# Loads of keys and queries, constants and search rounds at other places in an attention and mixture-of-experts kernel

## The chip, the cores and the metric

The kernel runs on one core of a Trainium2 chip. A core has engines that work side by side, each through its own list of instructions in order: TensorE (PE, with its weight loads as PEld), VectorE (DVE), ScalarE (ACT), GpSimd (POOL) and SyncE (SP), which here does nothing but issue DMAs. The metric is the device time of one execution in microseconds (us).

## The reference

Attention over 8 batches of 8 heads, 576 positions and 64 dimensions. Heads 0 to 3 see the last 32 positions (local), heads 4 to 7 every 32nd position (strided). Its output is read as 4608 tokens of 512 values, which 8 experts share out: all token-expert pairs are walked in order of falling logit, and an expert is closed when it has 576 tokens.

```python
    scores = scale * np.matmul(q, k.transpose(0, 1, 3, 2))
    mask_local = (rel >= 0) & (rel < stride)
    mask_strided = (rel >= 0) & (pos[None, :] % stride == pos[:, None] % stride)
    scores = np.where(masks[None, :, :, :], scores, -1000000000.0)
    ...
    return np.matmul(attn, v).astype(np.float32)
```

```python
    cap = N // E
    logits = x @ w_gate
    order = np.argsort(-logits.flatten())
    for idx in order:
        tok, e = (int(idx) // E, int(idx) % E)
        if assigned[tok] >= 0 or counts[e] >= cap:
            continue
        assigned[tok] = e
        counts[e] += 1
    for e in range(E):
        mask = assigned == e
        out[mask] = np.maximum(x[mask] @ w1[e], 0.0) @ w2[e]
```

## The kernel before

**Attention.** The work is cut into 16 units, one for each batch and kind (strided, local, strided, ...); a unit has two pairs of heads, p = 0 and 1. The loop of steps i runs from -1 to 31 (L597). In step i the kernel finishes the scores of pair i + 1 (`close_scores`, `max_t`, `shift`), multiplies the probabilities of pair i with the values (`mix`, L390) and normalizes (`norm`), and opens the scores of pair i + 2 (`open_scores`: `masks` L336, `dots` L347). Four steps make one batch. Gate logits of finished batches, transposes of x and stores of x to a scratch in HBM (`store`, L417 to 429) lie in between. In this part the order on all engines is the order of the code (`tc.manual_schedule()`).

**Loads.** SP issues the loads in the code's order. `flow` (L259) issues a group of transfers; its first one waits for a named instruction (`mark`), or, without a mark, until the group three before has landed. `load_kq` brings the keys and queries of one pair (two transfers of 288 to 304 KB), `load_v` half the values of a unit. Ahead of the loop stand units 0 and 1 in full, the values and the keys and queries of unit 2, and the gate weights. In step i the loop then loads for unit i//2 + 3: half the values at the start of an even step and half in its middle, the keys and queries of pair 0 at its end, of pair 1 in the middle of the odd step. The six constants that routing needs, and desc8h, are issued in step 13 (`CONST_AT`, `late_constants` L169). They are read from `summit` (desc8h, from step 24 on) and from the routing after the loop (the others).

**Routing.** After the last logits the first expert's threshold is found alone (`first_round`, `search0`). An expert is the one that fills up first, so experts are found one after the other: `side` (L1126) searches the threshold of expert ph (`search`), numbers its tokens (`slots`), issues its weight loads (`weights`), starts its index and gather work (`fetch`: `indices`, `tokens`), and strikes its tokens out before the next search. A search has seven rounds. A round compares all logits with 17 thresholds (VectorE `cm` L811), counts by matmul (TensorE L827), sums (VectorE L830, L833), counts again (TensorE L836), compares with the capacity (VectorE L843) and adds up (TensorE L846).

**Experts.** `ffn` (L1177) does the two layers of an expert in float16 halves, L1167 for the first layer, L1209 and L1215 for the second. TensorE's order is written by hand here (`MAN`), that of the other engines comes from a scheduler by priority. All the side work is cut into chains (generators). The planner keeps a clock in ns: each matmul of `ffn` adds its cost (123, 216 or 108), and between two matmuls every chain that is due is taken one step on (L1267 to 1271). What a chain yields is the time until its next step. So in a search T_COUNT = 2950 stands between `cm` and the count L827, T_SUM = 1350 between the count and L836, T_STEP = 1225 between L836 and L846; for the search beside the first expert (one expert closed) they are multiplied by PACE1. T_HOT = 4200 (T_HOT1 = 6350 for ph = 1) stands between the index tables and the index matmul L955. Larger numbers move a matmul later in TensorE's order; too small ones make TensorE wait for the operand.

An expert's `ffn` starts when its chain has set `ready`; the splits of its weights that aren't out by then are put out at once (`rush`). Weights of expert ph are asked for only when `ffn` of ph - 2 is written out (L1132). The split weights have two buffers, the loaded ones one.

Of the kernel before, what the change touches and what calls it, by code (L numbers as in the profile page):

```python
# [19 lines left out]
N, DM, E, FF = B * S, H * D, 8, 1024  # L20
# [8 lines left out]
NB = S // 32  # L29
BANK = 512  # L30
OPEN_S, OPEN_L = 1, 3
CONST_AT = 13
DEPTH = 3
MAX_FIRST = True
WARM = {(-2, 0): 11, (-1, 0): 3, (-1, 2): 3, (31, 0): 2}
# [13 lines left out]
URGENT = 4000  # L49
T_FIRST, T_COUNT, T_SUM, T_STEP, T_PREFIX, T_NEXT, T_HOT, T_DUP, T_LOAD = 1100, 2950, 1350, 1225, 3900, 2300, 4200, 550, 8000  # L50
PACE1 = 0.55
H0 = 256
HURRY = (0, 1, 7)
MAN, MAN0, MANP = {mybir.EngineType.PE}, {mybir.EngineType.Activation}, (0,)
T_W20, T_STEP0 = 9000, 1000
X1 = 100
# [3 lines left out]
T_F, T_LOAD0, T_HOT1, T_W, T_SQ, T_SCALE, T_CUT, T_BULK0 = 3000, 1500, 6350, 4000, 1500, 1500, 1500, 600  # L60
# [77 lines left out]
def band_stride_attention_then_capacity_moe(ctx, tc, qt, kl, ks, nl, ns, wg, w1, w2, cst, out, dbg=None):  # L138
    nc = tc.nc
# [15 lines left out]
    wg_sb = const.tile([128, H // 2, E], F32, name="wg_sb")  # L155
    sum_g = const.tile([128, E], F32, name="sum_g")
# [9 lines left out]
    ones_j = const.tile([128, 128], F16, name="ones_j")  # L166
    nc.vector.memset(ones_j, 1.0)

    def late_constants():  # L169
        for t, name in ((desc8h, "desc_h"), (fold, "fold"), (small, "small"), (tri, "tri"), (pick, "pick"), (iota, "iota")):  # L170
            split_of = {"iota": NC, "pick": 2 * NT}.get(name)
            nc.sync.dma_start(t, cst[name].rearrange("q (s c) -> q s c", c=split_of) if split_of else cst[name])
        nc.sync.dma_start(val[:, :2], cst["val"].rearrange("q (a c) -> q a c", a=2))

    ident_b = const.tile([128, 128], BF16, name="ident_b")
    nc.vector.tensor_copy(ident_b, ident)
# [43 lines left out]
    with tc.tile_pool(name="ld", bufs=2) as ld, \  # L220
# [336 lines left out]
                u.load_v(f)  # L557
        for f in range(2):
            todo[2].load_v(f)
        for p in range(2):  # L560
            todo[2].load_kq(p)
        flow([(wg_sb, wg), (sum_g, cst["sum_g"])])
        last = 2 * nu - 1
        edge = (B - 2) * S // TP

# [31 lines left out]
        for i in range(-1, 2 * nu):  # L597
            u, n, m = pair(i), pair(i + 1), pair(i + 2)
            nu_ = todo[i // 2 + 3] if i >= 0 and i // 2 + 3 < nu else None
            if nu_ and i % 2 == 0:  # L600
                nu_.load_v(0, todo[0].top if i == 0 else todo[i // 2 - 1].done)
            if i == CONST_AT:
                late_constants()
            if n:
                close_scores(n)
            if 2 < i < last:
                x = pair(i - 1)
                x[0].turn(x[1])
            warm(i, 0)
            for f in drips.get(i, []):  # L610
                f()
            for f in squares.get(i, []):
                f()
            if m or i in mids:
                a = room(m) if m else ps_a.tile([128, 2, 512], F32, name="spa")
            if i in mids or i in mids2 or i in mids3:
                b = ps_b.tile([128, 512], F32, name="spb")
            if u:
                if u[1] == 0:
                    u[0].begin()  # L620
                if i < last:
                    u[0].mix(u[1], 0)
            if i < last:
                for f in mids.get(i, []):
                    f(a, b)
            if i == last:
                pt = [ps_a.tile([128, 2, 512], F32, name="spa") for _ in range(2)]
                p1 = ps_b.tile([128, 512], F32, name="spb")
                for ts_, p_ in zip(parts, (None, p1)):
                    for h in range(2):  # L630
                        u[0].mix(u[1], h, ts_, p_)
                    u[0].norm(u[1], ts_, p_)
                break
            if n and MAX_FIRST:
                n[0].max_t(n[1])
            if nu_ and i % 2 == 0:
                nu_.load_v(1, n[0].top)
            elif nu_:
                nu_.load_kq(1, n[0].top)
            if u:  # L640
                u[0].mix(u[1], 1)
            if n and not MAX_FIRST:
                n[0].max_t(n[1])
            warm(i, 1)
            if m:
                open_scores(m)
            warm(i, 2)
            if u:
                u[0].norm(u[1])
            if nu_ and i % 2 == 0:  # L650
                nu_.load_kq(0, u[0].done)
            if i in mids2 and i > 1:
                mids2[i].total_v(b)
            for f in mids3.get(i, []):
                f(a, b)
            if n:
                n[0].shift(n[1])
            warm(i, 3)
            if i == -1:
                todo[0].square_v()  # L660
            if i == 1:
                todo[1].total_v(b)
                todo[1].scale_v()
            if i in FIRST_AT:
                todo[0].turn(FIRST_AT.index(i))
            for f in late.get(i, []) + fills.get(i, []):
                f()
# [129 lines left out]
                    nc.tensor.matmul(pm[:, :E], ones_j[:J], g, start=True, stop=True)  # L797
                    return settle(pm[:, :E], top, grid[:, rd, J0:])

    def pace(t):  # L800
        return t if len(closed) > 1 else t * PACE1

    def search(rm, ohc, more):
        cand, src, top = cand0, rm, None
        ohv = ohc.rearrange("p c e -> p (c e)")
        for rd in range(R1):
            last = rd == R1 - 1
            t = cand[:, :J1] if last else cand[:, 1:J1 + 1]
            with urgent():
                cm = rt.tile([TP, NC, J1], F16, name="cm")  # L810
                nc.vector.tensor_tensor(cm, src[:, :, None].to_broadcast([TP, NC, J1]),  # L811
                                        t[:, None, :].to_broadcast([TP, NC, J1]), op=OP.is_ge)
                cv = cm.rearrange("p c j -> p (c j)")
                n = 1 if rd == R1 - 2 else J1 + 1
                if not last:
                    pre = cand[:, 0:1]
                    if n > 1:
                        pre = rt.tile([128, n], F32, name="pre1")
                        nc.vector.tensor_scalar(pre, steps[:, rd + 1, :n], cand[:, 0:1], None, op0=OP.add)
                if rd == 0:  # L820
                    more()
            yield pace(T_COUNT) + (X1 if len(closed) == 1 else T_FIRST if rd == 0 else 0)
            with urgent():
                pr = ps_r.tile([128, 512], F32, name="pr_")
                pc, p2, pm = pr[:GC * J1, :GC * E], pr[:, 64:64 + E], pr[:, 128:128 + (E if last else 1)]
                for k in range(0, NC, GC):
                    nc.tensor.matmul(pc, cv[:, k * J1:(k + GC) * J1], ohv[:, k * E:(k + GC) * E], start=(k == 0),  # L827
                                     stop=(k == NC - GC))
                red = rt.tile([GC * J1, GC, E], F16, name="red")
                nc.vector.tensor_tensor(red.rearrange("p c e -> p (c e)"), pc, fold[:, :GC * E], op=OP.mult)  # L830
                r8 = rt.tile([GC * J1, E], F16, name="r8")
                with nc.allow_low_precision(reason="whole numbers up to 1152"):
                    nc.vector.tensor_reduce(r8, red.rearrange("p c e -> p e c"), axis=AX.X, op=OP.add)  # L833
            yield pace(T_SUM)
            with urgent():
                nc.tensor.matmul(p2, fold[:, GC * E:], r8, start=True, stop=True, skip_group_check=True)  # L836
                g = rt.tile([128, E], F16, name="g1")
                ih = rt.tile([128, 1], F16, name="ih1")
                if last:
                    nc.vector.tensor_scalar(g, p2, float(CAP), None, op0=OP.is_ge)  # L840
                else:
                    with nc.allow_low_precision(reason="zero or one"):
                        nc.vector.tensor_scalar(g, p2, float(CAP), 0.0, op0=OP.is_ge, op1=OP.max, accum_out=ih)  # L843
            yield pace(T_STEP)
            with urgent():
                nc.tensor.matmul(pm, ones_j, g if last else ih, start=True, stop=True, skip_group_check=True)  # L846
                if not last:
                    cand = rt.tile([128, n], F32, name=f"cand{n}")
                    nc.vector.scalar_tensor_tensor(cand, steps[:, rd, J1 + 1:].to_broadcast([128, n]), pm, pre,
                                                   op0=OP.mult, op1=OP.add)  # L850
                if rd == R1 - 2:
                    top, src = cand, rt.tile([TP, NC], F32, name="rml")
                    nc.vector.tensor_scalar(src, rm, top, None, op0=OP.subtract)
                    cand = steps[:, rd + 1, :J1 + 1]
        with urgent():
            return settle(pm, top, steps[:, R1 - 1, J1 + 1:])
# [72 lines left out]
    def indices(ph, slot):  # L929
        hurry = ph in HURRY  # L930
        with urgent(ph) if hurry else nullcontext():
# [13 lines left out]
            for h in range(3):  # L945
# [1 line left out]
                nc.vector.tensor_tensor(o, sh[:, 1:2, h * nh:h * nh + nh].to_broadcast([TP, SLO, nh]),  # L947
                                        iota[:, :, :nh], op=OP.is_equal)
                ohl.append(o)
        yield T_HOT1 if ph == 1 else T_HOT  # L950
        with urgent(ph):
            pi = ps_r.tile([128, 512], F32, name="pr_")
            for c in range(NC):
# [385 lines left out]
```

## Time and profile before

| what | us |
|---|---|
| runs shown, median (lowest to highest) | 696.55 (696.18 to 700.16) |
| profiled execution, its own time | 693.16 |
| its span | 691.4 |

| stretch, us | TensorE busy, us | VectorE busy, us | granted clock | DMA share |
|---|---|---|---|---|
| 0 to 190, attention | 170.73 | 135.13 | 0.94 | 0.76 |
| 190 to 236, last logits and first search | 29.73 | 30.95 | 0.67 | 0.27 |
| 236 to 578, six experts and a part of the seventh | 315.93 | 255.43 | 0.99 | 0.50 |
| 578 to 692, the rest | 99.35 | 38.61 | 0.93 | 0.27 |

How to read the profile: a row of the timeline has the start, the duration, the engine, the line, the operation, `out<-in`, and the count; the bracket gives the idle time before it and what ended it, where "issue" means that the engine waited for nothing that the profile shows. A row of the waits has the waiting engine and line, what it waited for, and the total, the number and the longest in us. The granted clock is the share of full speed that TensorE was given; the DMA share is the mean busy share of the core's 16 DMA engines.

### The profile page before, as it was taken

What the parts mean: (1) busy time and instruction counts of PE and PEld (TensorE: products, weight loads), DVE (VectorE), ACT (ScalarE), POOL (GpSimd) and SP (SyncE); (2) the same over time, 40 slices, a digit from 0 to 9 for tenths busy, and PEclk for the clock granted to TensorE, in tenths of its full rate; (3) what the DMA queues carried; (4) which work ended last, traced back from release to release, by engine and by line L of the source; (5) the groups of instructions that cost most, each with busy time, mean ns of one, the idle gap of its engine ahead of it and who ended that gap; (6) DMA issues with size and microseconds to landing.
All of it is one profiled execution on the core that took longest, in us unless ns stands there. A gap on an engine that the chain in (4) does not pass through costs nothing.

```text
span 691.4 us, 19758 instructions
## 1 busy us (share of the span) xinstructions
PE 615.7 (89%) x8294; PEld 404.1 (58%) x8298; DVE 460.1 (67%) x1389; ACT 330.6 (48%) x551; POOL 111.5 (16%) x124
## 2 busy tenths in 40 slices
PE   8789998999964789989989979989999998999993
PEld 4567776766743465457448537547646744745741
DVE  4857776787857879786776777777778656580200
ACT  2443643464410644772762564484385277771210
POOL 2100110111000200410340140051042041211011
PEclk9898998999965899999999999999999998999997
DMA  8996888795210821860870770590293188731010
GB/s 233 250 256 176 249 234 212 212 265 162 68 41 2 271 65 35 306 109 1 298 153 1 264 172 16 177 241 33 105 270 78 60 276 236 221 59 50 1 39 31
DMA packets 76364, 102.42 MB, mean 148 GB/s; under 512 B 41292, under 2 KB 49062, under 8 KB 75763
## 3 DMA queue, kind: packets, MB, share of 16 engines
q1 hardware_dynamic: 68195, 79.61, 40.9%
q0 software_dynamic: 7360, 21.15, 9.9%
q8 instruction: 65, 1.06, 0.7%
q10 hardware_dynamic: 720, 0.39, 0.2%
q14 instruction: 24, 0.20, 0.1%
HBM read 73.60 MB, written 18.87 MB: 134 GB/s over the span
## 4 chain that ended last, share of the span: by engine, by line
PE 23%; issue 13%; DVE 10%; DMA 10%; POOL 4%; ACT 3%; SPq 1%; POOLq 0%; DVEq 0%; ACTq 0%
PE ph L1167 16%; DMA w<-in_w_dram 4%; DMA xr<-x_scr,idx 4%; PE ph L1215 3%; POOL xr L1072 3%; DVE w1l L1013 2%; DMA xt<-xg 2%; DVE w2l L1013 2%; POOL out_dram L1226 1%; DVE xg L1062 1%; DVE cm L811 1%; ACT jk L994 1%; PE ph L1209 1%; DVE hl L1175 1%; ACT xg L1061 1%
## 5 line engine op out<-in xcount | busy, mean ns | idle before, releaser
L1167 PE MATMUL ph<-xt,w1h 128*128 128x288 f16 (+2 forms) x1024 | 177.9, 289 | 6.4 <-DMA xt<-xg 4.1
L1167 PEld LDWEIGHTS <-w1h 128*128 128x128 f16 x1024 | 97.6, 99 | 37.8 <-issue 7.7
L1167 PE MATMUL ph<-xt,w1l 128*128 128x288 f16 (+2 forms) x512 | 111.7, 289 | 0.0
L1226 POOL DMA_INDIRECT out_dram<-y,idx x40 | 49.6, 1239 | 332.5 <-ACT y L1225 304.4
L1215 PE MATMUL ph<-w2h,hh 128*128 128x512 f16 x256 | 97.0, 379 | 0.8 <-DVE hl L1175 0.8
L1215 PE MATMUL ph<-w2h,hl 128*128 128x512 f16 x256 | 97.0, 379 | 0.0
L1215 PE MATMUL ph<-w2l,hh 128*128 128x512 f16 x256 | 97.0, 379 | 0.0
L994 ACT ACTIVATE jk<-w 128x1024 f16<-128x1024 f32 x64 | 67.4, 1054 | 61.6 <-DMA w<-in_w_dram 60.6
L1174 ACT ACTIVATE hh<-ph 128x576 f16<-128x576 f32 (+2 forms) x72 | 42.6, 593 | 110.8 <-PE ph L1167 110.6
L1215 PEld LDWEIGHTS <-hh 128*128 128x128 f16 x512 | 49.1, 98 | 58.2 <-issue 7.8
L1175 DVE SCALAR_TENSOR_TENSOR hl<-ph,hh 128x576 f16<-128x576 f32 (+2 forms) x72 | 49.5, 687 | 47.4 <-ACT hh L1174 47.3
L1167 PEld LDWEIGHTS <-w1l 128*128 128x128 f16 x512 | 50.5, 99 | 14.1 <-issue 1.3
L373 ACT ACTIVATE pr<-spa 128x576 f32<-128x576 f32 x32 | 20.8, 650 | 72.0 <-PE spa L370 50.3
L1072 POOL DMA_INDIRECT xr<-x_scr,idx x40 | 41.8, 1045 | 53.3 <-DVE L L920 25.3
L1013 DVE SCALAR_TENSOR_TENSOR w1l<-w,w_sw,w1h 128x512 f16<-128x512 f32 x64 | 45.5, 744 | 4.7 <-ACT w1h L1012 4.5
L1215 PEld LDWEIGHTS <-hl 128*128 128x128 f16 x256 | 24.9, 97 | 39.3 <-issue 14.3
L1013 DVE SCALAR_TENSOR_TENSOR w2l<-w,w_sw,w2h 128x512 f16<-128x512 f32 x64 | 46.4, 744 | 1.8 <-ACT w2h L1012 1.6
L1012 ACT ACTIVATE w2h<-w,w_sw 128x512 f16<-128x512 f32 x64 | 41.2, 710 | 6.0 <-DVE w_sw L208 6.0
L1012 ACT ACTIVATE w1h<-w,w_sw 128x512 f16<-128x512 f32 x64 | 42.4, 708 | 3.2 <-DVE w_sw L208 2.1
L1225 ACT ACTIVATE y<-ph,so 128x512 f32<-128x512 f32 x32 | 21.7, 679 | 43.9 <-PE ph L1215 31.6
L424 POOL DMA_DIRECT2D x_scr<-xs x23 | 15.3, 670 | 168.0 <-DVE xs L408 125.2
L1062 DVE TENSOR_TENSOR xg<-xr,xg 128x512 f16<-128x512 f32 (+1 forms) x37 | 25.3, 687 | 18.5 <-ACT xg L1061 18.3
(603 smaller groups left out, 951.5 us busy)
## 6 DMA issues: line engine op xcount, KB each, us to landing
w<-in_w_dram SPq DMA_DIRECT2D x64, 512.0 KB
kl<-in_kl_dram SPq DMA_DIRECT2D x16, 304.0 KB
v_s<-in_ns_dram SPq DMA_DIRECT2D x16, 292.5 KB
v_l<-in_nl_dram SPq DMA_DIRECT2D x16, 292.5 KB
ks<-in_ks_dram SPq DMA_DIRECT2D x16, 288.0 KB
qs<-in_qt_dram SPq DMA_DIRECT2D x16, 288.0 KB
ql<-in_qt_dram SPq DMA_DIRECT2D x16, 288.0 KB
x_scr<-xl SPq DMA_DIRECT2D x8, 512.0 KB
```

The lines of the kernel that those rows point to most:

```text
L373: nc.scalar.activation(pr[:, :S].rearrange("k (h n) -> k h n", h=2), u.sp[p][:, :, :HS], AF.Exp, scale=0.125)
L994: nc.scalar.activation(jk, wf[:, c * n4:(c + 1) * n4].rearrange("p c f -> p (c f)"), AF.Square, scale=1.41422, accum_out=sq[:, c:c + 1])
L1012: nc.scalar.activation(hi[:, c, f], wf[:, c, f], AF.Copy, scale=s_)
L1013: nc.vector.scalar_tensor_tensor(lo[:, c, f], wf[:, c, f], s_, hi[:, c, f], op0=OP.mult, op1=OP.subtract)
L1062: nc.vector.tensor_tensor(xs[:, 1], xv, xs[:, 0], op=OP.subtract)
L1072: nc.gpsimd.indirect_dma_start(out=xr[:n], out_offset=None, in_=x_rows, in_offset=bass.IndirectOffsetOnAxis(ap=idx[:n, t:t + 1], axis=0))
L1167: nc.tensor.matmul(tile_[:, j, :w], wt[:, d, f * 128:(f + 1) * 128], xt[:, d // 2, xx, d % 2, c], start=(k == 0), stop=(k == 3 * DC - 1))
L1174: nc.scalar.activation(hv, src, AF.Relu)
L1175: nc.vector.scalar_tensor_tensor(lv, src, 0.0, hv, op0=OP.max, op1=OP.subtract)
L1215: nc.tensor.matmul(py, a[:, f, ts_], w[:, f], start=(k == 0), stop=(k == len(todo) - 1))
L1225: nc.scalar.activation(y, py, AF.Copy, scale=so[:, t:t + 1])
L1226: st = nc.gpsimd.indirect_dma_start(out=out_rows, out_offset=bass.IndirectOffsetOnAxis(ap=idx[:n, t:t + 1], axis=0), in_=y[:n], in_offset= ...
```

## The change

Three edits in the attention part: the loop loads the keys and queries of unit i//2 + 2 in place of i//2 + 3, and the ones of unit 2 no longer stand ahead of the loop; desc8h goes with the gate weights; the other constants leave step 13 and are issued at the start of steps 26 (small, fold), 27 (tri, pick, val) and 28 (iota). Three in the planner: for searches with more than one expert closed, the waits of rounds 4, 5 and 6 are multiplied by 0.72; T_SUM of rounds 1 and 2 gets 1000 more; the eighth expert's index matmul waits for T_HOT1 in place of T_HOT.

```diff
-CONST_AT = 13
...
+PACE, CROWDED, T_MORE = (1, 1, 1, 1, 0.72, 0.72, 0.72), (1, 2), 1000
...
-    def late_constants():
-        for t, name in ((desc8h, "desc_h"), (fold, "fold"), (small, "small"), (tri, "tri"), (pick, "pick"), (iota, "iota")):
+    def late_constants(i):
+        for t, name in {26: ((small, "small"), (fold, "fold")), 27: ((tri, "tri"), (pick, "pick")), 28: ((iota, "iota"),)}.get(i, ()):
...
-        nc.sync.dma_start(val[:, :2], cst["val"].rearrange("q (a c) -> q a c", a=2))
+        if i == 27:
+            nc.sync.dma_start(val[:, :2], cst["val"].rearrange("q (a c) -> q a c", a=2))
...
-        for p in range(2):
-            todo[2].load_kq(p)
-        flow([(wg_sb, wg), (sum_g, cst["sum_g"])])
+        flow([(wg_sb, wg), (sum_g, cst["sum_g"]), (desc8h, cst["desc_h"])])
...
+            kq_ = todo[i // 2 + 2] if i >= 0 and i // 2 + 2 < nu else None
...
-            if i == CONST_AT:
-                late_constants()
+            late_constants(i)
...
-            elif nu_:
-                nu_.load_kq(1, n[0].top)
+            elif kq_ and i % 2:
+                kq_.load_kq(1, n[0].top)
...
-            if nu_ and i % 2 == 0:
-                nu_.load_kq(0, u[0].done)
+            if kq_ and i % 2 == 0:
+                kq_.load_kq(0, u[0].done)
...
-    def pace(t):
-        return t if len(closed) > 1 else t * PACE1
+    def pace(t, rd):
+        return t * PACE[rd] if len(closed) > 1 else t * PACE1
...
-            yield pace(T_COUNT) + (X1 if len(closed) == 1 else T_FIRST if rd == 0 else 0)
+            yield pace(T_COUNT, rd) + (X1 if len(closed) == 1 else T_FIRST if rd == 0 else 0)
...
-            yield pace(T_SUM)
+            yield pace(T_SUM, rd) + (T_MORE if len(closed) > 1 and rd in CROWDED else 0)
...
-            yield pace(T_STEP)
+            yield pace(T_STEP, rd)
...
-        yield T_HOT1 if ph == 1 else T_HOT
+        yield T_HOT1 if ph in (1, E - 1) else T_HOT
```

## The prediction

> **What bounds the kernel now.** I read the page's busy shares first, then windows over stretches of the run, then the waits of TensorE, and last the timelines around the longest of them.
>
> ```profile
> PE 615.7 (89%) x8294; PEld 404.1 (58%) x8298; DVE 460.1 (67%) x1389; ACT 330.6 (48%) x551; POOL 111.5 (16%) x124
> ...
> q8 instruction: 65, 1.06, 0.7%
> ```
>
> TensorE is busy for 89% of the span, and its order is written out by hand, so a wait on it is lost unless something later would have waited anyway. The change is worth what it removes of TensorE's idle time and of its slow time. Attention (up to 190 us) and the experts (from 236 us) have to be read apart, because they wait for different things.
>
> Attention first. Columns of the windows: length, busy time of each engine with its instructions, granted clock, DMA share, GB/s.
>
> ```profile
> 42.00:48.00 6.00, 4.35 (x126) 3.88 (x128) 2.46 (x6) 4.48 (x7) 0.00 (x0) 1.00 1.01 240
> 48.00:60.00 12.00, 12.00 (x250) 7.70 (x245) 6.50 (x17) 3.48 (x6) 1.84 (x3) 0.57 0.70 200
> 102.00:108.00 6.00, 3.62 (x96) 2.37 (x96) 3.33 (x9) 2.92 (x4) 0.00 (x0) 0.88 1.04 200
> 108.00:114.00 6.00, 6.00 (x106) 4.78 (x107) 3.24 (x14) 1.41 (x3) 0.00 (x0) 0.55 0.72 217
> 164.00:186.00 22.00, 19.90 (x590) 14.94 (x590) 16.81 (x51) 9.27 (x17) 1.84 (x3) 1.00 0.25 74
> ```
>
> ```profile
> 46.79 0.38 PE L390 MATMUL po<-v_s,pr 64*54 64x65 f32 x6 [1.65 <-issue]
> ...
> 106.36 0.53 PE L390 MATMUL po<-v_l,pr 64*32 64x65 f32 x15 [2.38 <-issue]
> ```
>
> Twice the DMA engines are full (shares 1.01 and 1.04), TensorE stops for 1.65 and 2.38 us with no releaser shown, and then it runs for 12 and 6 us at a granted clock of 0.57 and 0.55. The matmuls started by four such stops say what they are:
>
> ```profile
> 0.00:40.20 40.20, 31.73 (x727) 0.92 0.90 238
> 0.00:46.50 46.50, 36.50 (x854) 0.93 0.91 240
> 0.00:99.50 99.50, 87.62 (x2250) 0.91 0.84 231
> 0.00:106.00 106.00, 91.63 (x2378) 0.92 0.85 232
> ```
>
> The counts differ by 127, 1396 (11 times 126.9) and 128. A matmul comes with a weight load, so the stops stand at multiples of some 254 TensorE instructions. The page's instruction queue moved 1.06 MB in 65 packets, 16.3 KB each, and TensorE has 8294 + 8298 = 16592 instructions, 255 for each packet. I read the stops as refills of TensorE's instructions that arrive late while data transfers fill the DMA engines. What they cost, slow clock included, is seen in the length of a batch (four steps), marked by GpSimd's store:
>
> ```profile
> 50.48 1.84 POOL L424 DMA_DIRECT2D x_scr<-xs  x3 [20.47 <-DVE xs L408]
> 75.00 1.99 POOL L424 DMA_DIRECT2D x_scr<-xs  x3 [22.68 <-DVE xs L408]
> 95.87 2.19 POOL L424 DMA_DIRECT2D x_scr<-xs  x3 [18.88 <-DVE xs L408]
> 122.03 1.99 POOL L424 DMA_DIRECT2D x_scr<-xs  x3 [23.98 <-DVE xs L408]
> ```
>
> The batches take 24.52, 20.87 and 26.16 us. The middle one is the quiet case; the first is 3.65 and the last 5.29 us over it.
>
> Then the experts, by TensorE's waits from 280 to 635 us (total, times, longest):
>
> ```profile
> PE ph L1167 <- DMA xt<-xg: 4.1, 2, 3.0
> PE pr__6674 L836 <- DVE r L833: 2.8, 1, 2.8
> PE pr__7519 L836 <- DVE r L833: 1.8, 1, 1.8
> PE pr__5989 L836 <- DVE r L833: 1.7, 1, 1.7
> PE pr__9204 L955 <- DVE rv L941: 1.4, 1, 1.4
> PE pr__8284 L836 <- DVE r L833: 1.3, 1, 1.3
> PE pr__6754 L836 <- DVE r L833: 1.0, 1, 1.0
> ```
>
> The long ones are of three kinds: L836, the matmul behind a round's T_SUM, in rounds 1 and 2 of the searches for the fourth to seventh expert; the first matmul of the seventh expert, 3.0 us for its transposed tokens; and the eighth expert's index matmul, 1.4 us.
>
> **The change part by part.**
>
> *Late constants, step 13 to steps 26 to 28.* Six issues leave SP at 92 to 98 us and stand at 162 to 185 us instead; the seventh, desc8h (2 KB), goes with the gate weights at the start. By their shapes the six are 0.86 MB, and iota alone 0.59. In the old place they pile onto the loads of the next unit; the 2.38 us stop and the 0.55 clock follow. The bounds of the gain are 0 (the stop comes anyway) and the whole 5.29 us. I take 5.0, nearer the upper row, because no other batch from 75 to 95.87 us with the same loads shows such a stop. In the new place the share is 0.25; the constants and the last unit's keys and queries (1.18 MB by shape) add 2.0 MB, which at 240 GB/s is 8.5 us of 22, so the share becomes about 0.64, below the shares of 1.01 and 1.04 where the stops stand: cost 0, between 0 and another 2.38 us stop. On SP each issue takes about 0.35 us (row below), some 2 us in front of stores of x that nobody reads before the gathers of the first expert, after 190 us. The first reader of small is the grid behind the last logits, that of iota and val the slots behind the first search.
>
> *Keys and queries one unit later.* The same bytes, the same places in a step, but unit j takes the place of unit j + 1, so at every moment of the first half one unit, 1.18 MB or 4.9 us at 240 GB/s, has not been asked for. That thins the front, where the share is 1.01, and shifts nothing else. The gain lies between 0 and 6.8 us: 1.65 us of stop plus 12 us at clock 0.57, which lose 5.2. The batch's excess of 3.65 us is the nearer row, since it counts what reached the next batch; of it I take 2.5, as three of the four steps before 48 us keep their transfers. What covered the loads was distance; it shrinks to this:
>
> ```profile
> 19.62 0.35 SPq L260 DMA_DIRECT2D ks<-in_ks_dram  x1
> ...
> 40.20 0.82 SPq L260 DMA_DIRECT2D v_l<-in_nl_dram  x2
> 42.37 0.35 SPq L260 DMA_DIRECT2D kl<-in_kl_dram  x1
> ```
>
> ```profile
> 28.34 0.32 PE L347 MATMUL spa<-qs,ks 64*54 64x54 f32 x8
> ...
> 56.95 0.45 PE L347 MATMUL spa<-qs,ks 64*54 64x54 f32 x8
> ```
>
> ```profile
> 47.03 0.56 DVE L323 COPY v_l<-v_l 32x780 f32<-32x780 f32 x1 [2.22 <-DMA v_l<-in_nl_dram]
> ```
>
> At full DMA engines a load issued at 40.20 us landed by 47.03, in 6.8 us. In the steady part unit 4's keys will leave where unit 5's left, at 42.37 us, and are used at 56.95: 14.6 us, more than twice that. Only unit 2 is tight. Its keys left at 19.62 us; now three small loads and unit 3's values go ahead of them on SP, some 2.3 us, so about 21.9, and they are used at 28.34. That leaves 6.4 us against a landing of 6.8: cost 0.3, between 0 and the 2.3 us of the shift.
>
> *T_MORE, rounds 1 and 2.* L836 moves 1.0 us of planned matmul time later, and the clock of the experts is 1.00, so 1.0 us. TensorE does other work instead of waiting. Each of the waits of 2.8, 1.8, 1.7 and 1.3 us loses 1.0 and the one of 1.0 all of it: 5.0 us. Smaller ones aren't counted. Bounds: 0 (VectorE's own order shifts along) to 8.6, all five.
>
> *Rounds 4 to 6 at 0.72.* T_COUNT, T_SUM and T_STEP shrink from 5.525 to 3.978 us a round, 4.6 us a search, and with the 2.0 us added above a search is planned 2.6 us shorter. That is no gain by itself, since search runs beside the matmuls. The risk is that VectorE's answer isn't there:
>
> ```profile
> 373.34 0.20 DVE L833 TENSOR_REDUCE r<-red 68x8 f16<-68x32 f16 x1
> ```
>
> ```profile
> 374.27 0.17 PE L836 MATMUL pr__6248<-r,fold 68*128 68x8 f16 x1
> ```
>
> In round 5 the sum is done at 373.54 us, 0.73 before its matmul; T_SUM shrinks by 0.38. So a quiet round fits and one with a split or a relu (0.7 to 0.75 us on VectorE) ahead doesn't. Bounds over 15 rounds (five searches of three): 0 and 15 times 1.55, 23.2 us, all the shortening turned into waits. I take 0.2 us a round, 3.0, near the quiet row.
>
> *What follows from the shorter search.* Weights, indices and gathers of an expert follow the end of its search, so they come earlier by 2.6 us for the third expert and by more for each later one, since before, a search with its numbering (45.98 us planned) is about as long as an expert's matmuls (46.9) and afterwards 2.6 shorter. For the seventh expert the tokens come at least 2.6 and up to 13 us sooner, so its 3.0 us wait goes: 3.0. GpSimd's gathers then stand ahead of the scatters they queue behind now. The split weights go into the buffers of two experts before, which are free by then; the float buffer is free when the splits of the expert before are done, and that expert's start forces those.
>
> *T_HOT1 for the eighth expert.* L955 moves 2.15 us later; its 1.4 us wait goes, and the gather, with over 30 us to spare before that expert starts, comes 2 us later: 1.4, bounds 0 and 1.4.
>
> **The sum** against the profiled execution, 693.16 us: -5.0 -2.5 -5.0 -3.0 -1.4 +3.0 +0.3 = -13.6, so 679.6. The median of the runs shown is 3.4 us above the profiled execution; with that, 683.0 us.
>
> **A rule that speaks against it.** The Trainium skill, "Runtime: NRT & Kernel Launch", section "Instruction fetch mechanics", says that instructions come in 16 KiB blocks of 256 by a queue of the engine's own, and that this is mostly hidden because the next block is fetched while one runs. The block size agrees with the 127 matmuls above; "hidden" doesn't agree with the 2.38 us stop. By the rule moving data transfers would gain nothing in attention, and the sum would be that of rival 1.
>
> **The rivals.**
> 1. *The stops don't come from the data transfers.* Then they stay wherever the transfers stand, and both attention terms and the 0.3 go: -6.4, 690.2 us. For it: between the counts 854 and 2250 ten blocks pass without a long stop, with the same loads in the queues. Against: the two long stops lie in the two fullest windows. The page named just above would have it so.
> 2. *VectorE is late, not TensorE early.* The added 1.0 us moves the bulk work in VectorE's queue along with it and L836 waits as before; -8.6, 688.0 us. For it: VectorE's queue is in order and holds splits and token work between the two steps of a sum. Against: the work ahead of it waits for gathers, whose time the added delay doesn't move.
> 3. *Rounds 4 to 6 can't be shorter* (the other side). VectorE also has the splits of the next weights there, and as the search moves ahead of the experts it meets their burst at an expert's start. At 1.55 us in each of 15 rounds the sum is -13.6 - 3.0 + 23.2 = +6.6, 703.2 us. It ends slower from 16.6/15 = 1.1 us a round on. Against: round 5's 0.73 us to spare.
> 4. *More goes.* The whole slow stretch after 46 us goes (6.8 instead of 2.5) and no tight round waits: -20.9, 675.7 us.
>
> **How the numbers follow.** Forecast 0.50, rival 1 0.15, rival 2 0.12, rival 3 0.07, rival 4 0.16. The likeliest is 683.0, its own range 678 to 687. The range 672 to 693 takes in rivals 1, 2 and 4 with some 3 us for the spread of runs; rival 3 lies outside it. Within 1% (689.6 to 703.5 us) is about what a measurement of this kernel can't tell from no change. Faster takes the forecast, rivals 2 and 4: 0.78; the same takes rival 1 and half of rival 3: 0.18; slower 0.04.
>
> **What would show it.** In the changed profile: no stop of over 1 us on "issue" near 100 to 107 us and clock 0.9 or more in that stretch; batches of 21 to 22 us from 50 us on; no matmul of L347 released by a load but perhaps at 28 us; L836 waits of rounds 1 and 2 about 1 us shorter, and in rounds 4 to 6 waits that sum to about 3 us; no wait for xt at the seventh expert, none at the eighth's L955. Wrong it would be if the stops reappear at other blocks, above all at 164 to 186 us where the constants now are, or if L836, L846 and L827 of rounds 4 to 6 wait by 1 us each time.

## The result, and the profile after

The changed kernel takes 696.78 us, the kernel before 693.22 us (medians of 22 runs each, side by side). The ratio is 1.0065, with a 95% interval from 1.0041 to 1.0089: 4.5 us slower, between 2.8 and 6.2. The forecast was 683.0 us, with a range of 672 to 693. The ratios here and below count only executions within 1.5% of the fastest of the same kernel, which leaves out up to half of a series (6 of 12 for e2_kq), so medians of all executions stand beside them where that matters. The execution profiled in this series took 709.18 us, far above the median, so the profile read below is that of a second series of the changed kernel (e0_all), whose profiled execution took 692.03 us.

Attention first. These are the windows of the changed kernel cut at GpSimd's stores, one batch each (columns as in the prediction):

```profile
26.52:52.62 26.10, 21.99 (x489) 16.15 (x484) 16.05 (x45) 11.51 (x19) 2.18 (x4) 0.74 0.72 208
52.62:74.62 22.00, 20.22 (x610) 15.35 (x606) 16.38 (x47) 11.18 (x19) 2.10 (x3) 1.00 0.75 213
74.62:95.93 21.31, 20.02 (x606) 15.09 (x601) 16.64 (x47) 11.07 (x19) 1.99 (x4) 1.00 0.82 239
95.93:117.17 21.24, 20.33 (x595) 15.12 (x590) 16.34 (x47) 10.94 (x19) 1.99 (x4) 1.00 0.82 227
117.17:140.34 23.17, 21.46 (x582) 16.04 (x574) 16.73 (x47) 10.54 (x18) 2.12 (x4) 0.93 0.75 220
```

The batch that the constants left (95.93 to 117.17) took 26.16 us before and takes 21.24 now, at full clock. The one from 52.62 us fell from 24.52 to 22.00. But the first one grew from 22.65 to 26.10 at a clock of 0.74, and the one from 117.17 us from 20.94 to 23.17. TensorE's timeline in the first batch, with the wait in brackets, shows where:

```profile
28.62 0.44 PE L348 MATMUL spa<-qs,ks 64*54 64x54 f32 x8 [1.28 <-DMA qs<-in_qt_dram]
...
36.91 0.44 PE L391 MATMUL po<-v_l,pr 64*32 64x65 f32 x8 [2.83 <-issue]
```

Unit 2's queries are 1.28 us late, and a stop without a releaser stands at 36.91 us, where none stood before. TensorE has started 601 matmuls by then, 126 fewer than at the first of the prediction's four stops (727), so it is the block before that one. The same stretch in windows:

```profile
24.00:30.00 6.00, 4.55 (x100) 2.86 (x97) 5.77 (x14) 1.79 (x3) 2.17 (x3) 0.50 1.03 273
30.00:36.00 6.00, 4.07 (x113) 3.26 (x105) 2.65 (x8) 3.31 (x5) 0.00 (x0) 0.73 0.98 246
36.00:42.00 6.00, 5.09 (x77) 3.76 (x78) 1.89 (x5) 1.83 (x3) 0.00 (x0) 0.56 0.52 167
```

The DMA engines are as full as ever (1.03, 0.98), and the slow clock (0.50 to 0.73) now lasts from 24 to 42 us. Before, it stood at 24 to 30 us (0.66) and at 48 to 60.

Then the experts: TensorE's longest waits from 280 to 635 us (total, times, longest).

```profile
PE pr__8141 L845 <- DVE g L842: 2.8, 1, 2.8
PE pr__5893 L845 <- DVE g L842: 2.7, 1, 2.7
PE pr__7653 L835 <- DVE r L832: 1.6, 1, 1.6
...
PE pr__6648 L845 <- DVE g L842: 1.4, 1, 1.4
...
PE pr__7396 L845 <- DVE g L842: 1.3, 1, 1.3
...
PE pr__9228 L954 <- DVE rv L940: 1.0, 1, 1.0
PE ph L1166 <- DMA xt<-xg: 1.0, 1, 1.0
```

(In this file L835 is L836 of before, L845 is L846, L954 is L955.) The seventh expert's wait for its tokens is gone; the remaining 1.0 us stands at 297 us, at the second expert. The long waits on L836 in rounds 1 and 2 are gone too, but waits of 1.3 to 2.8 us stand on the matmul one step later in round 1 of four searches, for the comparison g. Before, that line waited 0.7 us in all.

### The profile page after: what moved, and what is told of

Same layout as the page of the kernel before. It is cut to its first block, busy times and chain, and to the rows that moved or that the text cites. A ratio compares the mean times of both kernels' runs of the same rounds, so it can differ in the third digit from the quotient of the medians.

```text
span 707.4 us, 19755 instructions
## 1 busy us (share of the span) xinstructions
PE 623.7 (88%) x8294; PEld 408.9 (58%) x8298; DVE 461.1 (65%) x1389; ACT 330.7 (47%) x551; POOL 108.5 (15%) x124
## 2 busy tenths in 40 slices
DMA packets 76364, 102.42 MB, mean 145 GB/s; under 512 B 41292, under 2 KB 49062, under 8 KB 75763
## 4 chain that ended last, share of the span: by engine, by line
PE 22%; issue 13%; DVE 10%; DMA 10%; ACT 4%; POOL 4%; SPq 1%; POOLq 0%; DVEq 0%; ACTq 0%
PE ph L1166 12%; PE ph L1214 7%; DMA w<-in_w_dram 5%; DMA xr<-x_scr,idx 4%; DVE w2l L1012 3%; POOL xr L1071 3%; ACT jk L993 2%; POOL out_dram L1225 1%; DVE w1l L1012 1%; DVE hl L1174 1%; ACT w2h L1011 1%; DVE cm L810 1%; PE ph L1208 1%; SPq L978 1%; ACT hh L1173 1%
## 5 line engine op out<-in xcount | busy, mean ns | idle before, releaser
L1225 POOL DMA_INDIRECT out_dram<-y,idx x40 | 45.0, 1126 | 265.6 <-ACT y L1224 244.9
L1071 POOL DMA_INDIRECT xr<-x_scr,idx x40 | 43.6, 1089 | 132.2 <-DVE idx L966 96.8
```

What stands on the lines that cost most here:

```text
L1071: nc.gpsimd.indirect_dma_start(out=xr[:n], out_offset=None, in_=x_rows, in_offset=bass.IndirectOffsetOnAxis(ap=idx[:n, t:t + 1], axis=0))
L1225: st = nc.gpsimd.indirect_dma_start(out=out_rows, out_offset=bass.IndirectOffsetOnAxis(ap=idx[:n, t:t + 1], axis=0), in_=y[:n], in_offset= ...
```

## The experiments

A ratio is to the kernel before on the same chip, with its 95% interval. A difference in us is that ratio's distance from 1 times the median of the kernel before in those runs (691 to 695 us).

**First split: the change again, and its parts.** e0_all is the whole change. e1_const (the constants, with desc8h at the gate weights) and e2_kq (keys and queries) have one of the two attention edits and the old planner, e3_search the three planner edits alone.

```diff
 # e1_const, of its lines
+            late_constants(i)
...
 # e2_kq, of its lines
+            kq_ = todo[i // 2 + 2] if i >= 0 and i // 2 + 2 < nu else None
...
 # e3_search, of its lines
+PACE, CROWDED, T_MORE = (1, 1, 1, 1, 0.72, 0.72, 0.72), (1, 2), 1000
...
+        yield T_HOT1 if ph in (1, E - 1) else T_HOT
```

> All parts of the change, once more, beside the three parts alone on the same chip. The sum measured over many runs was 0.65% slower (some 4.5 us). If the parts add up, the differences of e1, e2 and e3 sum to this one within 3 us. In the profile both theories expect two to five stops of over 0.5 us without a releaser in attention (late instruction refills), at other blocks than before.

> Only the constants move from step 13 to steps 26 to 28. Theory A (the prediction's: the stop at 106 us comes from the constants piling onto the loads): 4 to 5 us faster, the batch from 96 to 122 us shrinks from 26.2 to some 21 us. Theory B (refills come late at whichever block meets full DMA engines; the constants only chose the block): within 2 us of before, and a long stop stands elsewhere.

> Only the keys and queries move by one unit. Theory A: 2 to 3 us faster, the batch from 50 to 75 us shrinks from 24.5 to 22 us. Theory B: the first loads of unit 2 come too late, TensorE waits 1 to 2 us for them near 28 us, the clock falls in the first 50 us, and the time is 0 to 4 us longer.

> Only the planner's numbers change (rounds 4 to 6 at 0.72, T_MORE, T_HOT1). Theory A: 6 us faster (waits at L836 of rounds 1 and 2 shorter by 1 us each, no wait for xt at the seventh expert). Theory C: the wait goes on to the next matmul of the same round (L846 behind VectorE's comparison), since VectorE itself is late; tight rounds and the displaced side work add to it: 0 to 5 us slower.

| kernel | ratio | interval | median of all executions, us (before: 691.37) |
|---|---|---|---|
| e0_all | 0.9997 | 0.9953 to 1.0042 | 692.91 |
| e1_const | 0.9945 | 0.9907 to 0.9984 | 690.69 |
| e2_kq | 0.9877 | 0.9830 to 0.9923 | 688.86 |
| e3_search | 1.0131 | 1.0077 to 1.0184 | 701.84 |

By their ratios both attention edits gain; by the medians of all executions the gains are only 0.7 and 2.5 us. The planner edits lose 9.1 us, where the prediction had them gain 6.4 (−5.0 − 3.0 − 1.4 + 3.0). So the sign was lost in the searches. In this series the whole change shows no difference from before; its interval and that of the first series just touch.

The profiles of e1_const and e2_kq (executions of 700.24 and 694.88 us, above the medians of their kernels) bear on the question of the places. With the constants gone from step 13, e1_const still stops in the old place, 1.92 us at the same count of matmuls (2250) where before stopped for 0.82, and also in the new one:

```profile
100.92 0.32 PE L347 MATMUL spa<-qs,ks 64*54 64x54 f32 x8 [1.92 <-issue]
...
177.05 0.32 PE L390 MATMUL po<-v_l,pr 64*32 64x65 f32 x8 [1.33 <-issue]
```

Its batch from 95.47 us takes 25.37 us, not the 21 expected of theory A. The second stop (after 4155 matmuls, 15 times 127 behind 2250) comes while the DMA engines move nothing: their share was 0.80 to 1.01 from 164 to 174 us and 0.00 from 175 to 177. Why a block is late then stays open. In e2_kq the batch from 54.10 us shrinks to 21.76 us, as theory A said, and unit 2's queries come 0.86 us late with a clock of 0.50 to 0.78 from 24 to 48 us, as theory B said. With the constants still in step 13, keys that are now asked for behind them come 4.51 us late, at a place that the prediction called safe (only unit 2 was to be tight):

```profile
37.39 0.44 PE L390 MATMUL po<-v_l,pr 64*32 64x65 f32 x8 [3.10 <-issue]
...
106.67 0.38 PE L347 MATMUL spa<-qs,ks 64*54 64x18 f32 x6 [4.51 <-DMA ks<-in_ks_dram]
```

So in these profiles the two attention edits are not independent, and each alone is no clean measure of its term.

**Second split: the planner edits one by one, and the two attention edits together.**

```diff
 # f_more: T_MORE alone
+PACE, CROWDED, T_MORE = (1, 1, 1, 1, 1, 1, 1), (1, 2), 1000
 # f_pace: the factor 0.72 alone
+PACE, CROWDED, T_MORE = (1, 1, 1, 1, 0.72, 0.72, 0.72), (), 1000
 # f_hot: the eighth expert's wait alone
+        yield T_HOT1 if ph in (1, E - 1) else T_HOT
 # g_att: constants and keys and queries, planner as before
```

> The kernel before with T_MORE alone. Theory A (the prediction's): the waits at L836 of rounds 1 and 2 lose 1 us each, 4 to 5 us faster. Theory C: VectorE's comparison of the round is put one or two xg further back in its queue, behind gathers that haven't landed; the wait goes on to L846 at 2 to 3 us for each expert, and the time is 0 to 4 us longer than before.

> The kernel before with rounds 4 to 6 at 0.72 alone. The prediction's term: new waits of 3 us in rounds 4 to 6 against 3 us saved at the seventh expert's xt, so within 2 us of before. If the tight rounds cost more, 3 to 8 us slower with waits at L836 of round 4 of about 1 us for each expert.

> The kernel before with T_HOT1 for the eighth expert alone. The prediction's term: 1.4 us faster. If the later index matmul pushes the eighth expert's tokens into other work: 0 to 3 us slower.

> Constants and keys and queries moved, the planner's numbers as before. If the two attention parts add up and the planner's numbers are what costs, this is 1.2 to 1.9% faster than before (8 to 13 us); if the parts overlap (both remove the same congestion), about 1.2%.

f_more 1.0099 (1.0055 to 1.0143), f_pace 1.0044 (0.9995 to 1.0093), f_hot 0.9958 (0.9919 to 0.9997), g_att 0.9951 (0.9910 to 0.9992). The medians of all executions are 703.10, 701.31, 693.87 and 693.67 us, against 695.21 before. T_MORE is the edit that loses: 6.9 us. By the ratios g_att gains less than e2_kq alone; the medians of all executions (1.5 and 2.5 us under before) don't tell the two apart.

**Which round does it, and are the gathers in the way?** m_more1 and h_more2 have T_MORE in one round each; o_nomore is the whole change without it; j_att_hot is g_att with f_hot's line, so the change without T_MORE and 0.72. In i_rows the halving of gathered tokens is planned 3 us later with the old planner otherwise, in m_rows the same together with T_MORE.

```diff
 # h_more2: CROWDED = (2,)   m_more1: CROWDED = (1,)   o_nomore, with 0.72: CROWDED = ()
+PACE, CROWDED, T_MORE = (1, 1, 1, 1, 1, 1, 1), (2,), 1000
 # i_rows and m_rows
-T_ROWS, T_ROW = 5000, 1200
+T_ROWS, T_ROW = 8000, 1200
```

> The kernel before with T_MORE in round 2 alone. f_more showed VectorE's comparison of round 1 set back behind gathers (L846 waits 1.7 to 2.4 us) and the distance between weight loads grown by 2.0 us for each expert. Theory C1 (what costs is the comparison of round 1 behind the gathers): without T_MORE in round 1 the L846 waits vanish and the time is within 2 us of before. Theory C2 (what costs is the longer chain of search, which sets the distance between experts): it grows by 1.0 instead of 2.0 us for each expert, and half of f_more's loss stays, 3 to 4 us.

> The kernel before with T_ROWS 8000 in place of 5000 (the halves of the gathered tokens stand 3 us later in the planner's time; ready stays where it was). Theory C1: VectorE no longer meets gathers that haven't landed between the two sums of round 1, the L836 waits of round 1 (0.5 to 2.8 us) vanish, 2 to 5 us faster, unless the transposed tokens come too late for the next expert, which would show as waits for xt of 2 to 3 us each and 0 to 10 us slower.

> Constants and keys and queries moved and T_HOT1 for the eighth expert, the search as before: the parts that were not slower alone. If they add up, 0.7 to 1.0% faster than before (5 to 7 us).

> The kernel before with T_MORE in round 1 alone. Theory C1 (the comparison of round 1 falls behind gathers): waits at L846 of round 1 of 1.7 to 2.4 us as with both rounds, and 4 to 7 us slower than before. Theory C2 (the length of the search chain): half of the loss with both rounds, about 3 us, whichever round it is.

> The kernel before with T_MORE in rounds 1 and 2, and with T_ROWS 8000. The halves of the gathered tokens stand behind round 1 again. Theory C1: no wait over 1 us at L846 of round 1 and most of the 6.9 us of T_MORE gone, within 3 us of before. Theory C2: still 5 to 8 us slower, since the search chain is as long as with T_MORE alone.

> The whole change without T_MORE. If T_MORE is the step that turned the change slower: 0.3 to 0.9% faster than before. If the shorter rounds 4 to 6 do it: within 0.3% of before or slower.

| kernel | ratio | interval |
|---|---|---|
| h_more2, round 2 alone | 0.9992 | 0.9934 to 1.0050 |
| m_more1, round 1 alone | 1.0057 | 1.0012 to 1.0101 |
| m_rows | 1.0275 | 1.0208 to 1.0342 |
| i_rows | 0.9970 | 0.9908 to 1.0033 |
| o_nomore | 0.9989 | 0.9947 to 1.0030 |
| j_att_hot | 0.9923 | 0.9870 to 0.9976 |

T_MORE in round 1 alone loses 4.0 us, in round 2 alone no difference is seen; but the two intervals overlap, and by the medians of all executions both are 2.4 us above before, so the times alone don't settle the round. The waits do: in round 1 the matmul of g waits for 0.5 to 3.3 us in four searches of m_more1, and for 1.2 us once in all of h_more2. i_rows shows no difference, and it is no test: in its trace the halves of the gathered tokens still stand between the two sums of round 1 and between the sum and the comparison. j_att_hot holds the moves that gained: 5.3 us faster than before by the ratio, 3.2 by the medians of all six executions (690.85 against 694.04).

o_nomore differs from j_att_hot by the factor 0.72 alone. It was expected to be faster than before and by the ratio isn't. The intervals of the two overlap, and by the medians of all executions o_nomore is 3.1 us under before (691.98 against 695.03), as far as j_att_hot; f_pace points to a loss. Nor does o_nomore settle what T_MORE costs within the whole change: that kernel with T_MORE stood at 0.9997 in one series and 1.0065 in the other. Waits of o_nomore, then of j_att_hot, from 280 to 640 us:

```profile
PE pr__6621 L845 <- DVE g L842: 3.0, 1, 3.0
PE pr__5886 L835 <- DVE xg L1061: 2.3, 1, 2.3
...
PE ph L1166 <- DMA xt<-xg: 1.2, 1, 1.2
```

```profile
PE ph L1165 <- DMA xt<-xg: 5.6, 3, 2.6
...
PE pr__6674 L834 <- DVE r L831: 2.0, 1, 2.0
```

The tokens' waits fall from 5.6 to 1.2 us, and round 1 waits longer (its matmuls are L835 and L845 in o_nomore, L834 in j_att_hot): 8.1 us for VectorE over the searches, against 4.2 and two stops of 3.1 without a releaser. The last weight load in SP's timeline, in the same order:

```profile
562.68 15.87 SPq L978 DMA_DIRECT2D w<-in_w_dram  x8
```

```profile
575.79 12.39 SPq L977 DMA_DIRECT2D w<-in_w_dram  x8
```

It comes 13.1 us earlier, and the span ends at 689.1 us, against 686.6: in these two profiles the searches run further ahead of the experts with 0.72, and the end doesn't follow. That the search holds the experts back is not borne out here.

m_rows missed and tells nothing about the gathers. It was expected to move the halves behind the comparison; in its trace they still stood ahead of it. Its experts also start before their tokens, with T_ROWS at 8000 leaving nothing between the last half and the start of the expert (T_LOAD − T_ROWS is 0). In i_rows, with the same 0, those waits come to 5.9 us only, so it takes T_MORE too:

```profile
PE ph L1168 <- DMA xt<-xg: 19.5, 10, 4.1
```

**Do the transfers hold up the refills?** k_noload is the kernel before without the key and query loads from unit 4 on: units 4 to 15 read what units 0 to 3 brought, so their scores, and the routing after them, are those of other data. It leaves out 12 units of 1.18 to 1.21 MB each, 14.4 MB in all (102.42 against 88.06 MB moved).

```diff
+                j = todo.index(u)
+                if j >= 4:
+                    u.kt, u.q = todo[j % 4].kt, todo[j % 4].q
+                    return
```

> The kernel before without the loads of keys and queries from unit 4 on (those units read the ones of units 0 to 3, so scores and the routing are of other data); 14 MB less on the DMA engines from 30 to 165 us, the same instructions on TensorE. Theory B (instruction refills come late because transfers fill the DMA engines): no stop without a releaser over 0.3 us after 45 us, and the all-reduce behind the last logits stands 6 to 12 us earlier than the 199 to 209 us of the kernels with attention as before. If the refills are late for another reason, the stops at multiples of 127 matmuls stay and the all-reduce moves by under 3 us.

The ratio is 0.9781 (0.9713 to 0.9849), 15.2 us. Windows of k_noload, then of the kernel before:

```profile
48.00:102.00 54.00, 51.37 (x1535) 38.50 (x1531) 43.08 (x126) 28.74 (x47) 5.21 (x8) 1.00 0.54 140
102.00:150.00 48.00, 46.12 (x1327) 35.59 (x1328) 37.69 (x108) 25.40 (x41) 3.84 (x6) 0.98 0.47 124
```

```profile
48.00:102.00 54.00, 51.94 (x1428) 37.71 (x1423) 39.27 (x111) 25.62 (x42) 6.02 (x9) 0.91 0.78 226
102.00:150.00 48.00, 44.20 (x1216) 33.13 (x1218) 34.63 (x96) 23.43 (x39) 3.98 (x6) 0.93 0.81 224
```

In the same 102 us TensorE gets through 2862 matmuls rather than 2644, with a clock of 1.00 and 0.98 instead of 0.91 and 0.93. And these are all the stops without a releaser from 20 to 200 us, in k_noload and in the kernel before:

```profile
PE po L394 <- issue: 0.9, 2, 0.6
PE spa L351 <- issue: 0.3, 1, 0.3
```

```profile
PE po L390 <- issue: 5.9, 5, 2.4
PE spa L347 <- issue: 2.3, 3, 0.9
PE spa L357 <- issue: 0.2, 1, 0.2
```

## Why the prediction was wrong, point by point

Each term of the sum beside its edit measured alone, by the ratios (the second and third rows of the prediction's experts, 0.72 and the tokens, are one edit):

| term | forecast, us | measured, us | interval |
|---|---|---|---|
| constants, keys and queries, unit 2 | −7.2 | −3.4 (g_att) | −6.3 to −0.6 |
| T_MORE | −5.0 | +6.9 (f_more) | +3.8 to +9.9 |
| tokens −3.0, tight rounds +3.0 | 0 | +3.1 (f_pace) | −0.3 to +6.5 |
| T_HOT1 | −1.4 | −2.9 (f_hot) | −5.6 to −0.2 |
| sum | −13.6 | +3.7 | whole change: +2.8 to +6.2 |

The forecast also added 3.4 us for the base, as the three runs of the kernel before that were shown lay above its profiled execution; the median of 22 runs was 693.22 us, so that term came out at 0.1 us.

**The step that failed is T_MORE,** in the sentence "TensorE does other work instead of waiting" and in the argument against rival 2, "the work ahead of it waits for gathers, whose time the added delay doesn't move". L836 did wait less. But the next step of the round, the comparison g that L846 needs, slid behind more of that gather work. VectorE's timeline before, in round 1 of two searches that follow one another (pr__5909 and pr__6674):

```profile
347.18 0.20 DVE L833 TENSOR_REDUCE r<-red 68x8 f16<-68x32 f16 x1
348.07 0.69 DVE L1062 TENSOR_TENSOR xg<-xr,xg 128x512 f16<-128x512 f32 x1 [0.69 <-ACT xg L1061]
348.68 0.16 DVE L843 TENSOR_SCALAR_CACHE_REDUCE g<-pr__5909 128x8 f16<-128x8 f32 x1
...
401.84 0.18 DVE L830 TENSOR_TENSOR red<-pr__6674,fold 68x32 f16<-68x32 f32 x1
403.96 0.69 DVE L1062 TENSOR_TENSOR xg<-xr,xg 128x512 f16<-128x512 f32 x1 [1.93 <-ACT xg L1061]
404.57 0.20 DVE L833 TENSOR_REDUCE r<-red 68x8 f16<-68x32 f16 x1
404.68 0.68 DVE L1062 TENSOR_TENSOR xg<-xr,xg 128x512 f16<-128x512 f32 x1
405.28 0.16 DVE L843 TENSOR_SCALAR_CACHE_REDUCE g<-pr__6674 128x8 f16<-128x8 f32 x1
```

and after (e0_all), in the same round and search as the first three rows:

```profile
340.55 0.19 DVE L832 TENSOR_REDUCE r<-red 68x8 f16<-68x32 f16 x1
341.36 0.69 DVE L1061 TENSOR_TENSOR xg<-xr,xg 128x512 f16<-128x512 f32 x1 [0.62 <-ACT xg L1060]
343.53 0.69 DVE L1061 TENSOR_TENSOR xg<-xr,xg 128x512 f16<-128x512 f32 x1 [1.48 <-ACT xg L1060]
344.14 0.75 DVE L1012 SCALAR_TENSOR_TENSOR w1l<-w,w_sw,w1h 128x512 f16<-128x512 f32 x1
344.80 0.16 DVE L842 TENSOR_SCALAR_CACHE_REDUCE g<-pr__5893 128x8 f16<-128x8 f32 x1
```

Each xg here is VectorE's half of a gathered tile. Where it waits, it is for ScalarE's half of the same tile, and that waits for the gather:

```profile
342.87 0.63 ACT L1060 ACTIVATE xg<-xr 128x512 f16<-128x512 f32 x1 [1.54 <-DMA xr<-x_scr,idx]
```

The xg that waits for 1.93 us ahead of the sum of pr__6674 is what made L836 late before. Before, one xg stands between the sum r and the comparison g: 1.50 us from start to start in the first search, 0.71 in the second. After, two that wait and a split stand there: 4.25 us in the first search, and 2.92 in the second (one xg that waits for 1.46 us, and a split). TensorE, which reaches L846 as before T_STEP after L836, pays for it:

```profile
345.02 0.16 PE L845 MATMUL pr__5893<-ih,ones_j 128*128 128x1 f16 x1 [2.67 <-DVE g L842]
```

That the wait moved with T_MORE and didn't go holds from kernel to kernel. Sums of the waits of L836 for r (or an xg) and of L846 for g, 280 to 640 us, worked out from the rows of the waits view, stops without a releaser left out:

| kernels | L836, us | L846, us |
|---|---|---|
| T_MORE in round 1 (e0_all, e3_search, m_more1, m_rows) | 0.6 to 7.4 | 6.7 to 8.6 |
| not in round 1 (before, f_hot, g_att, h_more2, i_rows, j_att_hot, o_nomore) | 7.2 to 12.7 | 0.0 to 3.0 |

Leaving out m_rows, the two columns together come to 13.9 us on average in the first group and 11.0 in the second; with the stops without a releaser on these two lines it is 14.0 and 12.5. So rival 2 had the mechanism, at another place than it named, and its price of 0 was too low by some 1.5 to 3 us. f_more itself, with 6.9 us at L836 and 8.3 at L846, fits the first group. The time that T_MORE costs, 6.9 us or at least 3.8, is more than these waits. That the search as a whole gets longer and the next expert's weights later was the other theory. From the second to the seventh expert the weight loads are 57.5 us apart in f_more, 55.1 in the kernel before, but also 56.8 in f_hot, whose numbers in these searches are those of before, so it is neither shown nor excluded. That part stays open.

**Attention: half the size, and the two terms can't be told apart.** Lengths of the first five batches between the stores, as means over the profiles of seven kernels with the old order (before, e3_search, f_hot, h_more2, i_rows, m_more1, m_rows), four with the new one (e0_all, g_att, j_att_hot, o_nomore), and of k_noload:

| kernels | 1 | 2 | 3 | 4 | 5 |
|---|---|---|---|---|---|
| old order | 23.1 | 23.2 | 21.3 | 25.6 | 21.7 |
| new order | 24.6 | 22.1 | 21.0 | 21.2 | 22.5 |
| k_noload | 19.4 | 21.3 | 20.6 | 20.6 | 21.0 |

The constants' batch (4) lost 4.4 us (its lowest of the seven old ones is 23.75, the highest of the four new ones 21.4), near the 5.0 forecast. But this is with both edits: e1_const, with the constants alone, took 25.37 us there, and the first profile of the changed kernel (709.18 us) 24.46, so that moving the constants by itself does it is not shown. The new place, 164 to 186 us, had a share of 0.55 in e0_all, 0.64 forecast, and no stop; the stop of e1_const at 177.05 us, where that stretch has a share of 0.51, says that the cost there was not always 0. The term of keys and queries was mis-sized: 1.1 us gained in batch 2, as against 2.5, and 1.5 lost in batch 1, as against 0.3. That 1.5 is a mean of two kinds: batch 1 took 26.1 and 26.4 us in e0_all and g_att, 22.9 and 23.0 in the two others. The failed step is "That thins the front [...] and shifts nothing else": the DMA engines stay full from 24 to 36 us, and the stop and the slow clock can come earlier; the forecast had only unit 2's own lateness there (1.28 us found, 0.3 forecast). Over all seven batches the new order gains 3.8 us on average, which agrees with g_att. With f_more and f_pace counted among the old, and the first profile of the changed kernel among the new, it is 1.9.

Rival 1, that the stops don't come from the transfers, is refuted for the attention part as a whole by k_noload: the share falls to about 0.5 and the stops with it. Single stops can have another cause, as the one of e1_const with idle DMA engines. That they are late refills is still read from their places: the stop at 36.91 us and the five of e0_all over 0.5 us behind it (58.78, 77.33, 99.75, 119.36 and 162.57 us) stand at counts of 601, 1110, 1617, 2252, 2759 and 3902 matmuls, all multiples of some 127 apart. The Trainium skill, "Runtime: NRT & Kernel Launch", section "Instruction fetch mechanics", which speaks of mostly hidden fetches, agrees with this kernel at that share only; at 0.8 it doesn't. What the prediction missed is that asking for 1.18 MB later leaves the share high, and then other blocks are late.

**The tokens and the tight rounds.** The wait of 3.0 us for the seventh expert's tokens went wherever 0.72 was in (1.2 us of xt waits left in o_nomore, 1.0 in e0_all, 1.7 in f_pace). Rounds 4 to 6 of e0_all wait for some 3.4 us in all, 3.0 forecast, with 1.6 us the longest (L835 above), and all of it in round 4. Not forecast was that an end of the search 13 us earlier gives nothing back, and that round 1, whose matmuls then meet other work, waits up to 3.0 us. The interval of f_pace reaches from no change to a loss.

**T_HOT1** took its wait away, as said: no such row in f_hot or j_att_hot. In the whole change 1.0 us is left. The 2.9 us of f_hot are over the bound of 1.4, but their interval holds it.

The range was too narrow on the side of a loss because rival 3, the only slower one, was about rounds 4 to 6, and T_MORE's least gain was put at 0, though no trace row excluded a loss.

## What to carry to other kernels

When a matmul waits on an in-order engine, look at what stands ahead of the producer and what that waits for. Delaying the matmul can let the scheduler put more of that work ahead of the next producer, and then the wait moves one step on, as from L836 to L846 here. The long stops of this kernel went when its DMA share fell to 0.5 (k_noload), and came at other blocks when bytes were only shifted: ask what the share is afterwards in every stretch that the bytes pass through. And where an edit changes the order of a queue that no trace shows yet, give its term a bound on the side of a loss too.

## What was not expected of the hardware

Attention with the same order of instructions ended between 199.1 and 209.9 us in the profiles of seven kernels (204.5 in that of the kernel before): which stops are long differs from run to run, so one profile doesn't weigh an edit of 3 us there. The same goes for the rest: from there to the end of the span it was 486.5 to 494.0 us in six profiles with the searches' numbers as before (before, e1_const, e2_kq, f_hot, g_att, j_att_hot). Without the loads attention ended at 190.3 us, so the loads of units 4 to 15, by their stops and slow clock above all, cost some 14 us of 204.
